# A new beginning for an attention and two-MLP kernel: other head pairs, loads on two queues, splits on three engines, the first group earlier

## The chip, the cores and the metric

The kernel runs on one core of one Trainium2 chip, as one program. The metric is the device time of that program in microseconds (us), the median of several runs. The engines are named as the profile names them: PE (TensorE), DVE (VectorE), ACT (ScalarE), POOL (GpSimd) and SP (SyncE, which here only issues DMAs).

## The reference

Attention with heads mixed before and after the softmax (batch 4, 12 heads, 448 positions, head size 64), then two MLPs (1792 tokens, 768 to 2048 to 768), all in float32:

```python
scores = scale * np.matmul(q, k.transpose(0, 1, 3, 2))
scores = np.einsum('bhij,hg->bgij', scores, w_pre)
scores = scores - np.max(scores, axis=-1, keepdims=True)
attn = np.exp(scores)
attn = attn / (np.sum(attn, axis=-1, keepdims=True) + 1e-09)
attn = np.einsum('bhij,hg->bgij', attn, w_post)
out = np.matmul(attn, v)
h = x @ w_in                       # first MLP, x is out with heads side by side
g = np.where(h > 0.0, h, np.exp(np.minimum(h, 0.0)) - 1.0)
h = (g @ w_out) @ w_in2            # second MLP
y = np.maximum(h, 0.0) ** 2 @ w_out2
```

## The kernel before

A float32 operand is split in two parts, a rounded one (hi, float32r) and the remainder (lo = x - hi), and a product is made of three matmuls on the parts (two where one side is stacked). So every operand costs a copy to float32r and a subtraction before PE can use it.

The queries of a batch are cut in four chunks of 12, 11, 11 and 11 groups; a group is ten query rows with all twelve heads, 120 partitions. Four batches make 16 chunks and 180 groups. For a chunk n, `first_scores` (batch 0, two heads at a time in the two halves of the PE rows) or `scores` (later batches) writes score rows to PSUM, and copies bring them to the tile `sc[n]`. For a group t these steps follow, each on the engine named:

- `gather(t)`: SP issues a DMA from `sc[n]` to `graw`, which puts the 120 rows of the group together. It needs all twelve heads of the chunk. `graw` has 5 buffers.
- `split(t)`: ACT casts to `gh`, POOL (DVE for the first two groups) subtracts to `gl`.
- `mix_pre(t)`: three matmuls mix the heads. `maxima(t)`: DVE takes the negative maximum, ACT the exponential with its sum into `tot`.
- `weigh(t)`: for two groups at once DVE adds 1e-9 to `tot`, takes the reciprocal and scales the mixing weights `wg`.
- `mix_post(t)`: four matmuls, and DVE copies the result to `at`. `values(n, i)` multiplies by `v` when all groups of a chunk are in `at`.

The order is written out by hand (`manual_schedule`); each engine takes its instructions in program order. In step t of the loop at the end of `attention` stand the gather of group t + 9, the copies of finished scores, the split of t + 6, the maxima of t + 3, `mix_pre` of t + 4, scores of a later chunk, `mix_post` of t, and other work put beside it by the table `extra` (loads of k, q and v, splits of k and q, values). Every DMA of the kernel is issued by SP, and it takes the lane of the eighth DMA before it, for whose end it waits.

Ahead of the loop stands the beginning, which the change rewrites: 16 matmuls on a zero tile `idle`; loads of the keys of batch 0 (`k_room`) and of the queries of chunks 0 and 1 (`q_room`); for the six head pairs of chunk 0 the splits of k and q on DVE, the scores, and two copies by ACT; nine gathers; the same for chunk 1; the mixing weights (`prepare_mixes`); then splits, `mix_pre` and `maxima` of the first groups. `load_odd` writes a 0/1 pattern to DRAM and reads it back across partitions; `split_k` uses it. After attention the MLPs run, PE alone nearly without a pause.

Of the kernel before, what the change touches and what calls it, by code (L numbers as in the profile page):

```python
# [7 lines left out]
F32 = mybir.dt.float32  # L8
# [42 lines left out]
def attention(tc, dram, psum, qr, kr, vr, w_pre, w_post, diagonal, xd, mlps):  # L51
    nc = tc.nc
    with ExitStack() as ctx:
# [21 lines left out]
        def load_odd():  # L75
            for a in range(2):
                nc.gpsimd.memset(turns[:, :, a : a + 1], float(a))
            nc.sync.dma_start(out=turns_d, in_=turns.rearrange("o d a -> o (d a)"))
            nc.sync.dma_start(out=odd, in_=turns_d.rearrange("o p -> p o"))
# [37 lines left out]
        k_room = work.tile([128, 3, 2, S], F32, name="k_room", tag="at", bufs=2)  # L117
        q_room = work.tile([128, 2, H // 2, CH], F32, name="q_room", tag="v", bufs=3)
# [14 lines left out]
        def split_first_k(p):  # L133
            j, a = divmod(p, 2)
            if a == 0:
                k0[j] = [key_tile() for _ in "hl"]
            raw, (hi, lo) = k_room[:, j, a, :], (x[:, a, :] for x in k0[j])
            nc.vector.tensor_copy(hi, raw)
            nc.vector.tensor_tensor(lo, raw, hi.bitcast(F32), ALU.subtract)

        def first_q(n, i, raw=None):
            raw = q_room[:, n, 3 * i : 3 * i + 3, :] if raw is None else raw
            at = (n * H + 6 * i) * CH
            src = qr[0, :, at : at + 6 * CH].rearrange("d (p a i) -> d a p i", p=3, a=2)
            for a in range(2):
                nc.sync.dma_start(out=raw[64 * a : 64 * a + 64], in_=src[:, a])
# [8 lines left out]
        def split_first_q(n, i, engine=nc.gpsimd):  # L155
# [35 lines left out]
        def load_v(b, i):  # L191

            vt[b, i] = work.tile([NJ, JC, DM // 2], F32, name="v", bufs=3)
            src = vr[b].rearrange("j (c d) -> j c d", c=JC)
            nc.sync.dma_start(out=vt[b, i], in_=src[:, :, i * DM // 2 : (i + 1) * DM // 2])
# [583 lines left out]
```

## Time and profile before

| | us |
|---|---|
| median of 3 runs | 1390.31 (1389.82 to 1390.93) |
| the profiled execution | 1388.04 |
| its span | 1386.0 |

| engine | busy us | share of the span | instructions |
|---|---|---|---|
| PE | 1366.1 | 99% | 8764 |
| DVE | 865.1 | 62% | 1812 |
| ACT | 703.8 | 51% | 1578 |
| POOL | 304.1 | 22% | 285 |

Busy shares are means over the whole span. PE is the engine that is nearly always busy; an engine with a smaller share can still be the one waited for in some stretch, and that is read from the rows of that stretch. All times in rows count from the start of the span.

### The profile page before, as it was taken

Reading aid. Unit: us, or ns where it says so; the run is one execution under the profiler, and the core shown is the slowest. Engines: PE = TensorE matmul, PEld = TensorE weight load, DVE = VectorE, ACT = ScalarE, POOL = GpSimd, SP = SyncE. Lnnn points to the kernel's source line nnn. Section 1 sums busy time; section 2 is a strip of 40 time slices with the busy share of each in tenths; the row PEclk is TensorE's granted clock in tenths of the full one; section 3 lists DMA queues with packets and bytes.
Section 4 is the critical chain, followed back from the end, with each engine's and each line's share of the span. In section 5 each row is a group of like instructions: output and inputs, shape, how many; then the busy total and the mean of one; then the engine's idle time right before and its main releaser. Section 6 shows DMA issues by size and latency. Waiting matters only on the chain.

```text
span 1386.0 us, 23859 instructions
## 1 busy us (share of the span) xinstructions
PE 1366.1 (99%) x8764; PEld 1270.2 (92%) x8764; DVE 865.1 (62%) x1812; ACT 703.8 (51%) x1578; POOL 304.1 (22%) x285
## 2 busy tenths in 40 slices
PE   7999999999999999999999999999999999999998
PEld 4789999999987999999999999999999999999998
DVE  5777778878788799866599997634441223443121
ACT  5777877878766577532255553225551113443111
POOL 2776876777657000000000000000000000000000
PEclk8999999999999999999999999999999999999999
DMA  4744744753735455544355576532112111112131
GB/s 130 212 142 145 214 159 140 211 177 129 202 123 163 153 171 163 193 173 161 131 170 163 164 236 210 176 120 58 54 65 61 61 42 51 52 53 62 41 108 41
DMA packets 116217, 182.92 MB, mean 132 GB/s; under 512 B 26660, under 2 KB 94597, under 8 KB 116101
## 3 DMA queue, kind: packets, MB, share of 16 engines
q1 hardware_dynamic: 116101, 181.41, 41.3%
q8 instruction: 69, 1.13, 0.3%
q14 instruction: 47, 0.39, 0.1%
HBM read 106.48 MB, written 36.18 MB: 103 GB/s over the span
## 4 chain that ended last, share of the span: by engine, by line
PE 93%; DVE 2%; DMA 2%; ACT 1%; SPq 1%; POOL 1%; issue 1%; POOLq 0%; DVEq 0%; ACTq 0%
PE ps_post L288 9%; PE ps_mix L644 8%; PE ps_mix L646 8%; PE ps_mix L645 8%; PE ps_qk L646 6%; PE ps_post L646 6%; PE ps_post L644 6%; PE ps_qk L644 6%; PE ps_qk L645 6%; PE ps_post L645 6%; PE ps_pv L314 5%; PE ps_pv L646 3%; PE ps_pv L645 3%; PE ps_pv L644 3%; PE ps_mix L252 3%; PE ps_mix L254 2%
## 5 line engine op out<-in xcount | busy, mean ns | idle before, releaser
L525 ACT CAST wh<-wf 128x384 fp32r<-128x384 f32 (+1 forms) x240 | 126.8, 533 | 272.4 <-DVE wf L508 113.5
L532 DVE TENSOR_TENSOR wl<-wf,wh 128x384 fp32r<-128x384 f32 (+1 forms) x240 | 138.7, 581 | 157.2 <-ACT wh L525 153.3
L246 POOL TENSOR_TENSOR gl<-graw,gh 120x448 fp32r<-120x448 f32 x178 | 203.0, 1145 | 130.1 <-ACT gh L245 125.7
L288 PEld LDWEIGHTS ps_post<-wg,ex 120*112 120x112 f32 x1440 | 173.5, 178 | 18.2 <-issue 4.7
L288 PE MATMUL ps_post<-wg,ex 120*112 120x120 f32 x1440 | 180.4, 268 | 3.3 <-DVE wg L277 1.6
L264 ACT ACTIVATE ex<-ps_mix,nmax 120x448 f32<-120x448 f32 x180 | 117.6, 653 | 42.0 <-DVE nmax L260 41.9
L294 DVE COPY at<-ps_post 112x480 f32<-112x480 f32 x160 | 104.4, 653 | 35.6 <-PE ps_post L288 34.8
L245 ACT CAST gh<-graw 120x448 fp32r<-120x448 f32 x180 | 105.7, 590 | 27.7 <-POOL gl L246 9.3
L260 DVE TENSOR_REDUCE nmax<-ps_mix 120x1 f32<-120x448 f32 x180 | 111.0, 617 | 8.5 <-PE ps_mix L254 8.5
L644 PE MATMUL ps_mix<-xh,wh 128*128 128x448 f32 x288 | 104.5, 363 | 0.0
L645 PE MATMUL ps_mix<-xl,wh 128*128 128x448 f32 x288 | 104.4, 362 | 0.0
L646 PE MATMUL ps_mix<-xh,wl 128*128 128x448 f32 x288 | 104.4, 362 | 0.0
L302 ACT COPY sc<-ps_qk 120x448 f32<-120x448 f32 x168 | 86.3, 545 | 27.9 <-PE ps_qk L229 24.5
L252 PE MATMUL ps_mix<-gh,pre_l 120*120 120x448 f32 x180 | 81.5, 453 | 4.6 <-ACT gh L245 3.8
L666 DVE TENSOR_TENSOR tmp<-tmp 128x448 f32<-128x448 f32 x64 | 39.9, 624 | 69.8 <-ACT tmp L665 69.8
L314 PE MATMUL ps_pv<-at,v 112*64 112x110 f32 (+2 forms) x1488 | 78.2, 262 | 0.6 <-DVE at L296 0.6
L484 ACT ACTIVATE wf<-wd 128x384 f32<-128x384 f32 (+1 forms) x120 | 69.3, 578 | 15.2 <-DMA wd<-w1i 8.6
L314 PEld LDWEIGHTS ps_pv<-at,v 112*64 112x64 f32 x1488 | 71.6, 137 | 4.4 <-DVE at L296 0.8
L670 DVE TENSOR_TENSOR hl<-tmp,hh 128x448 fp32r<-128x448 f32 x128 | 74.1, 619 | 0.4
L508 DVE SCALAR_TENSOR_TENSOR wf<-wd,wf 128x384 int32<-128x384 int32 (+1 forms) x120 | 70.9, 591 | 4.1
L506 DVE SCALAR_TENSOR_TENSOR wf<-wd,wf 128x384 int32<-128x384 int32 (+1 forms) x120 | 70.3, 586 | 4.1
L644 PE MATMUL ps_post<-xh,wh 128*128 128x448 f32 x192 | 69.6, 362 | 0.0
(161 smaller groups left out, 3404.3 us busy)
## 6 DMA issues: line engine op xcount, KB each, us to landing
graw<-sc SPq DMA_DIRECT2D x180, 210.0 KB
wd<-w1i SPq DMA_DIRECT2D x32, 384.0 KB
wd<-w1o SPq DMA_DIRECT2D x24, 512.0 KB
wd<-w2i SPq DMA_DIRECT2D x32, 384.0 KB
wd<-w2o SPq DMA_DIRECT2D x32, 384.0 KB
qraw<-qr SPq DMA_DIRECT2D x48, 180.0 KB
kraw<-kr SPq DMA_DIRECT2D x36, 224.0 KB
w1if<-wf SPq DMA_DIRECT2D x32, 192.0 KB
```

Of the source, the lines that this page charges most:

```text
L245: nc.scalar.copy(hi, x)
L246: engine.tensor_tensor(lo, x, hi.bitcast(F32), ALU.subtract)
L252: nc.tensor.matmul(p, pre_l, hi, start=True, stop=False)
L260: nc.vector.tensor_reduce(nmax, p, AX.X, ALU.max, negate=True)
L264: nc.scalar.activation(e, p, AF.Exp, bias=nmax, scale=1.0, accum_out=tot[t // 2][:, t % 2 : t % 2 + 1])
L288: nc.tensor.matmul(p[:, c, :], e[:, c * NJ : (c + 1) * NJ], w, start=True, stop=True)
L314: nc.tensor.matmul(pv[n][o : o + 64, i % 3, :w], vt[b, i // 3][:, jc, g % 6 * D : (g % 6 + 1) * D], at[n][:, jc, g, :w], start=(jc == 0), ...
L525: nc.scalar.copy(hi, f)
L532: self.nc.vector.tensor_tensor(lo, self.single.pop(i), hi.bitcast(F32), ALU.subtract)
L644: mm(p, wh, xh, start=first, stop=False)
L645: mm(p, wh, xl, start=False, stop=False)
L646: mm(p, wl, xh, start=False, stop=last)
```

## The change

- Chunk 0 to 3 of batch 0: the two heads computed together are p and p + 6, where they were 2p and 2p + 1. So each half of a load is one contiguous piece of the source, and several pairs go in one DMA.
- The first four pairs of loads are issued half by SP and half by ACT. The queries of chunk 1 are loaded ahead of the mixing matrices, and the read-back of `odd` moves behind the first nine gathers.
- The splits of the beginning go to three engines: ACT casts the queries of chunk 0, POOL subtracts for them, for one key pair and for half of chunk 1's queries; DVE does the rest.
- Matmuls on `idle` stand ahead of head pairs 1 to 5 of chunk 0 (two each) and ahead of `mix_pre` 0 to 3 (5, 2, 2, 2): 21 in all. `idle` takes a buffer of `ex` and no longer one of `graw`.
- Of chunk 1, four head pairs come ahead of the first group; pairs 4 and 5 stand between the first groups' steps. `mix_post(0)` is ahead of the loop.
- `weigh` adds 1e-9 to each sum by an instruction of its own (one column); the weights of groups 0 and 1 are made one by one.
- `v` of a batch is loaded in 8 DMAs of a quarter each in 8 steps, where there were 2 whole ones in two steps.

```diff
-        def first_k(j, pairs):
-            src = kr[0, :, 4 * j * S : (4 * j + 4) * S].rearrange("d (p a j) -> d a p j", p=2, a=2)
-            for x, y in pairs:
-                for a in range(2):
-                    nc.sync.dma_start(out=k_room[64 * a : 64 * a + 64, j, x:y], in_=src[:, a, x:y])
+        def first_k(x, y, queues=(nc.sync, nc.sync)):
+            for a in range(2):
+                src = kr[0, :, (6 * a + x) * S : (6 * a + y) * S].rearrange("d (p j) -> d p j", j=S)
+                queues[a].dma_start(out=k_room[64 * a : 64 * a + 64, x:y, :], in_=src)
...
-            (nc.vector.tensor_copy if n < 2 else nc.scalar.copy)(hi, raw)
+            copy(hi, raw)
...
-        def load_v(b, i):
+        def load_v(b, i, c):
...
-            nc.sync.dma_start(out=vt[b, i], in_=src[:, :, i * DM // 2 : (i + 1) * DM // 2])
+            at = c * DM + i * DM // 2
+            nc.sync.dma_start(out=vt[b, i][:, c, :], in_=vr[b][:, at : at + DM // 2])
...
+            for _ in range(warm):
+                nc.tensor.matmul(banks[0], idle[:64, :128], idle[:64], start=True, stop=True)
...
-            nc.vector.tensor_scalar_add(both, both, 1e-9)
+            for i in range(n):
+                nc.vector.tensor_scalar_add(sums[:, i : i + 1], sums[:, i : i + 1], 1e-9)
...
-                put(first[n] + 3, load_v, b, 0)
-                put(first[n] + 4, load_v, b, 1)
+                for j in range(JC):
+                    put(first[n] + 2 * j + (1 if b == 0 else -4), load_v, b, 0, j)
+                    put(first[n] + 2 * j + (2 if b == 0 else 4), load_v, b, 1, j)
...
-        first_k(0, ((0, 1),))
-        first_q(0, 0)
-        first_k(0, ((1, 2),))
-        first_k(1, ((0, 2),))
+        two = nc.sync, nc.scalar
+        first_k(0, 1, two)
+        first_q(0, 0, queues=two)
+        first_k(1, 2, two)
+        first_k(2, 4, two)
         first_q(0, 1)
-        first_k(2, ((0, 2),))
+        first_k(4, 6)
+        for i in range(2):
+            first_q(1, i)
         load_mixes()
-        load_odd()
-        first_q(1, 0)
-        first_q(1, 1)
+        spread_turns()
+        split_first_q(0, 0)
         for p in range(6):
-            split_first_k(p)
-            if p % 3 == 0:
-                split_first_q(0, p // 3, nc.vector)
-            first_scores(0, p, tags[p % 4], (act, act), True)
+            split_first_k(p, nc.gpsimd if p == 4 else nc.vector)
+            if p == 1:
+                split_first_q(0, 1)
+            if p == 5:
+                split_first_q(1, 0, nc.vector, dve)
+                split_first_q(1, 1, nc.gpsimd, dve)
+            first_scores(0, p, tags[p % 4], (act, act), True, 2 if p else 0)
         for t in range(AHEAD):
             gather(t)
-        split_first_q(1, 0, nc.vector)
-        split_first_q(1, 1, nc.vector)
-        for p in range(6):
-            first_scores(1, p, tags[(p + 2) % 4], (act, act if p % 2 else dve), True)
+        load_odd()
         prepare_mixes()
-        for t in range(2):
-            split(t, nc.vector)
-        for t in range(MIX):
-            mix_pre(t)
-            if t < MAX:
-                maxima(t)
-            split(t + 2)
-        weigh(0)
+        for p in range(4):
+            first_scores(1, p, (("mix", "mix"), ("mix", "post"), ("post", "pv"), ("qk", "qk"))[p], (act, dve), True)
+        split(0, nc.vector)
+        split(1, nc.vector)
+        mix_pre(0, 5)
+        split(2)
+        split(3)
+        maxima(0)
+        mix_pre(1, 2)
+        maxima(1)
+        weigh_first(0)
+        first_scores(1, 4, ("post", "pv"))
+        mix_pre(2, 2)
+        split(4, nc.vector)
+        weigh_first(1)
+        mix_post(0)
+        keep_scores()
+        maxima(2)
+        first_scores(1, 5)
+        mix_pre(3, 2)
+        split(5)
```

ACT at the very start, before: it loads its table and then only copies scores (`sc_143` is chunk 0, L216 the copies).

```order
L216 ACT_TABLE_LOAD
L216 COPY sc_143<-ps_qk_144 120x448
L216 COPY sc_143<-ps_qk_145 120x448
L216 COPY sc_143<-ps_mix_156 120x448
L216 COPY sc_143<-ps_mix_157 120x448
```

The same place now (`sc_142` is chunk 0, L159 the cast of queries).

```order
L132 DMA k_room_91<-kr 64x448
L147 DMA q_room_92<-qr 64x360
L132 DMA k_room_91<-kr 64x896
L159 ACT_TABLE_LOAD
L159 CAST qp_134<-q_room_92 128x360
L221 COPY sc_142<-ps_qk_143 120x448
L221 COPY sc_142<-ps_qk_144 120x448
L159 CAST qp_155<-q_room_92 128x360
L221 COPY sc_142<-ps_mix_159 120x448
```

Four DMA issues (one of `k_room` 64x448 is left out as a repetition) and a cast stand ahead of the first copy, and a second cast behind the second copy.

ACT between the last copies of chunk 0 and the first exponential, before (`sc_248` is chunk 1, `graw_222` the first group, L245 the casts of groups).

```order
L216 COPY sc_143<-ps_mix_213 120x448
L216 COPY sc_248<-ps_post_249 120x448
L216 COPY sc_248<-ps_mix_259 120x448
L216 COPY sc_248<-ps_pv_260 120x448
L216 COPY sc_248<-ps_qk_269 120x448
L216 COPY sc_248<-ps_mix_279 120x448
L216 COPY sc_248<-ps_mix_280 120x448
L216 COPY sc_248<-ps_post_289 120x448
L216 COPY sc_248<-ps_mix_299 120x448
L216 COPY sc_248<-ps_pv_300 120x448
L245 CAST gh_316<-graw_222 120x448
L245 CAST gh_320<-graw_224 120x448
```

The same place now (`sc_265` is chunk 1, `graw_239` the first group, L250 the casts, L272 the exponentials).

```order
L221 COPY sc_142<-ps_mix_228 120x448
L221 COPY sc_265<-ps_mix_266 120x448
L221 COPY sc_265<-ps_mix_276 120x448
L221 COPY sc_265<-ps_post_286 120x448
L221 COPY sc_265<-ps_qk_296 120x448
L250 CAST gh_306<-graw_239 120x448
L250 CAST gh_310<-graw_241 120x448
L250 CAST gh_323<-graw_243 120x448
L250 CAST gh_327<-graw_245 120x448
L272 ACTIVATE ex_333,tot_334<-ps_mix_314,nmax_331 120x448
L272 ACTIVATE ex_344,tot_334<-ps_mix_336,nmax_342 120x448
L250 CAST gh_365<-graw_247 120x448
```

Nine copies of chunk 1 stood between the last copy of chunk 0 and the first group's cast; now there are four, and four casts stand ahead of the first exponential where there were two.

SP in steps 1 to 6 of the loop, before (`graw` is a gather, `kraw`, `qraw` and `v` are loads).

```order
L238 DMA graw_402<-sc_143 120x1x448
L162 DMA kraw_434<-kr 128x1x448
L238 DMA graw_436<-sc_143 120x1x448
L146 DMA qraw_456<-qr 64x3x120 x2
L238 DMA graw_459<-sc_248 120x1x448
L195 DMA v_491<-vr 112x4x384
L238 DMA graw_493<-sc_248 120x1x448
L162 DMA kraw_522<-kr 128x1x448
L195 DMA v_524<-vr 112x4x384
L238 DMA graw_526<-sc_248 120x1x448
```

The same place now.

```order
L243 DMA graw_427<-sc_142 120x1x448
L163 DMA kraw_459<-kr 128x1x448
L197 DMA v_461<-vr 112x384
L243 DMA graw_463<-sc_142 120x1x448
L147 DMA qraw_483<-qr 64x360 x2
L197 DMA v_486<-vr 112x384
L243 DMA graw_488<-sc_265 120x1x448
L197 DMA v_461<-vr 112x384
L243 DMA graw_522<-sc_265 120x1x448
L163 DMA kraw_551<-kr 128x1x448
L197 DMA v_486<-vr 112x384
L243 DMA graw_554<-sc_265 120x1x448
```

Between two gathers stands at most a quarter of a `v` tile, where a whole one stood twice; there are more issues in all.

## Rows read from the trace of the kernel before

**Rows 1.** Windows: start:end, length, busy of five engines, PE clock, DMA share, GB/s

```profile
0.00:60.00 60.00, 49.51 (x272) 33.48 (x273) 37.48 (x88) 38.31 (x90) 25.17 (x29) 0.89 0.61 170
60.00:1386.00 1326.00, 1316.62 (x8494) 1236.70 (x8492) 827.59 (x1725) 665.48 (x1489) 278.94 (x256) 1.00 0.41 130
```

**Rows 2.** Timeline of PE: start, length, what, idle before and its releaser

```profile
1.32 5.44 PE L376 MATMUL ps_pv<-idle 128*128 128x512 bf16 x16 [1.32 <-POOL idle L373]
...
6.70 0.88 PE L212 MATMUL ps_qk<-kp,qp 64*120 64x448 f32 x6
...
22.79 0.46 PE L252 MATMUL ps_mix<-gh,pre_l 120*120 120x448 f32 x1 [1.69 <-ACT gh L245]
...
29.71 0.73 PE L252 MATMUL ps_mix<-gh,pre_l 120*120 120x448 f32 x1 [0.81 <-ACT gh L245]
...
35.65 0.49 PE L252 MATMUL ps_mix<-gh,pre_l 120*120 120x448 f32 x1
...
36.38 0.98 PE L288 MATMUL ps_post<-wg,ex 120*112 120x120 f32 x8
...
37.82 0.98 PE L288 MATMUL ps_post<-wg,ex 120*112 120x120 f32 x8
...
39.34 0.87 PE L212 MATMUL ps_qk<-kp,qp 64*120 64x448 f32 x6
40.14 1.07 PE L288 MATMUL ps_post<-wg,ex 120*112 120x120 f32 x8
...
62.27 2.68 PE L314 MATMUL ps_pv<-at,v 112*64 112x120 f32 x48
```

**Rows 3.** Windows of one microsecond: length, busy PE, its clock, DMA share, GB/s

```profile
3.00:4.00 1.00, 1.00 (x4) 1.00 0.66 174
9.00:10.00 1.00, 0.24 (x2) 1.00 1.00 217
26.00:27.00 1.00, 0.94 (x2) 0.50 0.38 136
36.00:37.00 1.00, 1.00 (x10) 1.00 0.93 210
```

**Rows 4.** Timeline of SP's queue: issues of DMAs

```profile
0.75 1.25 SPq L131 DMA_DIRECT2D k_room<-kr  x2
...
16.54 12.36 SPq L238 DMA_DIRECT2D graw<-sc  x9
...
38.43 0.63 SPq L195 DMA_DIRECT2D v<-vr  x1
```

**Rows 5.** Timeline of DVE

```profile
4.13 0.39 DVE L138 CAST kp<-k_room 128x448 fp32r<-128x448 f32 x1 [4.13 <-DMA k_room<-kr]
...
28.36 0.16 DVE L272 TENSOR_SCALAR tot<-tot 120x2 f32<-120x2 f32 x1
...
28.76 0.58 DVE L277 TENSOR_SCALAR wg<-post,rec 120x120 f32<-120x120 f32 x2
```

**Rows 6.** Timeline of ACT

```profile
0.74 1.28 ACT L216 ACT_TABLE_LOAD   x1 [0.74 <-PEq L770]
...
15.54 0.97 ACT L216 COPY sc<-ps_mix 120x448 f32<-120x448 f32 x2
...
22.09 1.10 ACT L245 CAST gh<-graw 120x448 fp32r<-120x448 f32 x2
...
24.61 0.63 ACT L264 ACTIVATE ex<-ps_mix,nmax 120x448 f32<-120x448 f32 x1 [1.42 <-DVE nmax L260]
```

**Rows 7.** Timeline of POOL

```profile
25.86 2.23 POOL L246 TENSOR_TENSOR gl<-graw,gh 120x448 fp32r<-120x448 f32 x2 [24.43 <-ACT gh L245]
...
35.50 0.96 POOL L159 TENSOR_TENSOR qp<-qraw,qp 128x360 fp32r<-128x360 f32 x1 [1.33 <-ACT qp L158]
```

**Rows 8.** DMA rate in 40 slices of 15 to 20 us

```profile
GB/s 238 215 92 15 81 142 254 211 39 50 100 161 219 169 96 69 161 211 185 54 0 0 0 0 215 229 229 287 244 244 229 258 272 244 229 287 244 229 244 272
```

**Rows 9.** Chain of waits, 36 to 50 us

```profile
39.16 7.18 DMA graw<-sc
```

More of the change, by code (lines that the diff above doesn't have):

```diff
@@ L136, in split_first_k, with first_q @@
                 k0[j] = [key_tile() for _ in "hl"]
-            raw, (hi, lo) = k_room[:, j, a, :], (x[:, a, :] for x in k0[j])
+            raw, (hi, lo) = k_room[:, p, :], (x[:, a, :] for x in k0[j])
             nc.vector.tensor_copy(hi, raw)
[L139 to L144, printed above, removed]
+            engine.tensor_tensor(lo, raw, hi.bitcast(F32), ALU.subtract)
+        def first_q(n, i, raw=None, queues=(nc.sync, nc.sync)):
+            raw = q_room[:, n, i, :, :] if raw is None else raw
             for a in range(2):
-                nc.sync.dma_start(out=raw[64 * a : 64 * a + 64], in_=src[:, a])
+                at = (n * H + 6 * a + 3 * i) * CH
+                src = qr[0, :, at : at + 3 * CH].rearrange("d (p i) -> d p i", p=3)
+                queues[a].dma_start(out=raw[64 * a : 64 * a + 64], in_=src)
             qraw[n, i] = raw
@@ L201, in score_tile, with first_scores @@
             sc[n] = score[(n + 1) % 2].tile([CH, H, S], F32, name="sc", bufs=1)
-        def first_scores(n, p, tags=("qk", "qk"), copies=(nc.scalar.copy, nc.scalar.copy), now=False):
+        def first_scores(n, p, tags=("qk", "qk"), copies=(nc.scalar.copy, nc.scalar.copy), now=False, warm=0):
             if p == 0:
                 score_tile(n)
-            out = [bank(psum, tag)[:CH, :S] for tag in tags]
+            banks = [bank(psum, tag) for tag in tags]
+            out = [x[:CH, :S] for x in banks]
+            for _ in range(warm):
+                nc.tensor.matmul(banks[0], idle[:64, :128], idle[:64], start=True, stop=True)
             h, l = 0, 1
@@ L215, in first_scores @@
                 for a in range(2):
-                    copies[a](sc[n][:, 2 * p + a, :], out[a])
+                    copies[a](sc[n][:, 6 * a + p, :], out[a])
             else:
-                taken.extend((sc[n][:, 2 * p + a, :], out[a]) for a in range(2))
+                taken.extend((sc[n][:, 6 * a + p, :], out[a]) for a in range(2))
         def scores(n, h):
@@ L247, in split, with mix_pre @@
             parts[t] = hi, lo
-        def mix_pre(t):
-            p = bank(psum, "mix")[:120, :S]
+        def mix_pre(t, warm=0):
+            p = bank(psum, "mix")
+            for _ in range(warm):
+                nc.tensor.matmul(p, idle[:, :128], idle, start=True, stop=True)
+            p = p[:120, :S]
             hi, lo = parts.pop(t)
@@ L267, in weigh, with weigh_first, weigh_some @@
         def weigh(t):
-            if t % 2 or t >= T:
-                return
-            both = tot.pop(t // 2)
-            nc.vector.tensor_scalar_add(both, both, 1e-9)
+            if t % 2 == 0 and t < T:
+                weigh_some(t, tot.pop(t // 2))
+        def weigh_first(t):
+            weigh_some(t, tot[0][:, t : t + 1])
+        def weigh_some(t, sums):
+            n = sums.shape[1]
+            for i in range(n):
+                nc.vector.tensor_scalar_add(sums[:, i : i + 1], sums[:, i : i + 1], 1e-9)
             rec = work.tile([120, 2], F32, name="rec", bufs=2)
-            nc.vector.reciprocal(rec, both)
-            for i in range(2):
+            nc.vector.reciprocal(rec[:, :n], sums)
+            for i in range(n):
                 w = work.tile([120, 120], F32, name="wg", bufs=4)
```

19 lines of the change are left out of this document (10 added, 9 removed).

## The prediction

> **What bounds the kernel now.** I read four things in turn. First the windows: from 60 us to the end PE is busy 1316.6 of 1326.0 us at a granted clock of 1.00, in the first 60 us only 49.5 and at 0.89 [rows 1]. So the change can win only in the first 60 us, and what it wins there comes off the end whole, as long as PE finds its work ready afterwards; 9.4 us of idling is all that is left behind 60 us. Second, PE's timeline of the beginning, for stations that both kernels pass: 16 idle matmuls to 6.76, the first scores at 6.70, the first `mix_pre` at 22.79 behind a wait for ACT's cast, `mix_pre(4)` at 29.71, `mix_pre(6)` at 35.65, and `values` of chunk 0 at 62.27 [rows 2]. Third, the other engines at those stations, to see what they wait for. Fourth, the windows of single microseconds: PE is granted 0.50 (1.2 of 2.4 GHz) at 26 us, 3 us behind the wait of 1.69 that ended at 22.79, and has 1.00 again at 36 us [rows 2, 3]. `mix_pre(4)` to `mix_pre(6)` is the PE work of two groups; it took 5.94 us, where a group at full clock takes 37.82 - 36.38 = 1.44 us [rows 2]. So the low clock costs 5.94 - 2.88 = 3.1 us there.
>
> I add up four stretches, each from one station to the next, on the profiled execution's clock.
>
> **Stretch 1, to the end of chunk 0's copies.** Before: ACT's last two copies start at 15.54 and take 0.97, end 16.51 [rows 6]. Now ACT first issues four loads. An issue by SP took 0.62 (two in 1.25) and the pair landed at 4.13, 2.13 after the second issue's end [rows 4, 5]; ACT's own issues are not in the trace, and I take the same 0.62. The first queries are then issued by 2.0 on both queues and land at about 4.1. The table load waits for them, 1.28, to 5.4; the cast takes at most 0.55 (two of 448 columns took 1.10), to 5.95 [rows 6]; POOL's subtraction 0.96, to 6.9 [rows 7]. PE is busy with idle matmuls to 6.76 anyway, and the first pair takes 0.88 [rows 2]: its end stays near 7.6. From there ACT makes six pairs of copies of 0.97 and one more cast, 6.4 us, and with 0.05 allowed between instructions it ends at 14.3. PE keeps that pace: two idle matmuls and a pair. An idle matmul took 0.34 on average [rows 2], mostly at low clock; at full clock I estimate 0.21, and 0.43 + 0.60 stays near 0.97. The loads keep it too, just: DMA moved 174 GB/s at a share of 0.66 at 3 us, where one queue issued, and 217 at 1.00 at 9 us [rows 3]; the second queue fills the first stretch and no more, so the last keys come about 1 us earlier than before. Gain 16.5 - 14.3 = 2.2. Bounds: nothing, if loads or ACT's issues are slower than SP's, and 2.2.
>
> The Trainium skill ("ScalarE: Activation LUTs", What ACT_TABLE_LOAD costs) counts 1.28 us for the load and 1.38 more for a drain, 2.66. The row shows 1.28, as the page has it; ACT then waited, so a drain could hide behind it. With the drain the first pair would come 1.2 us later and the gain be 1.0.
>
> **Stretch 2, to the cast of group 0.** Before: 16.51 to 22.09, 5.6 us, because ACT had its nine copies of chunk 1 ahead of the cast [rows 6]. The data were there long before: the gather was issued at 16.54 [rows 4], its bytes began to move at 18.0 and five gathers moved at about 250 GB/s [rows 8], so 0.86 us each, and the first was complete by 18.9; with 0.2 for its signal that is 2.5 us after the issue. Now ACT has four copies ahead, 2.1 us, which fit beneath those 2.5. DVE's four lie beside them. Gain 3.1; the cast starts at 16.8. Bounds: 2.0 if the landing takes a microsecond more, 3.4.
>
> **Stretch 3, to `mix_pre(6)`.** Before 13.6 us (22.09 to 35.65). Now four casts stand ahead of the first exponential, and the fourth group lands 3 x 0.86 later, at 19.4: cast to 20.0, exponential 0.63 [rows 6] to 20.6, add, reciprocal and first weights 0.7 (28.36 to 29.05 [rows 5]) to 21.3. PE does `mix_post(0)` (0.82 of the 1.44) to 22.1, pair 5 of chunk 1 (0.80, 39.34 to 40.14 [rows 2]), idle matmuls and two `mix_pre` by 24.6. The longer branch runs over ACT: DVE's second weights and maximum 2 to 23.5, exponential 24.1, cast 5 24.7, POOL 1.12 [rows 7] to 25.9, and over two copies and cast 6 at 26.2 POOL again to 27.3. So `mix_pre(6)` lies at 27.1 rather than 35.65, 10.3 us behind the cast. Gain 3.3, which is nearly the 3.1 of the low clock: with 11 idle matmuls PE has no pause above 1 us in my chain. Bounds: 0, if the clock falls as before, and 4.
>
> **Stretch 4, to `values` of chunk 0.** Before 62.27 - 35.65 = 26.6. The PE work in it is 12 groups of 1.44 and six pairs of 0.80, 22.1, so 4.5 were lost. The chain names the loss: a gather of 39.16 took 7.18 us to land [rows 9], with a whole `v` tile issued just ahead of it at 38.43 [rows 4] and DMA at a share of 0.93 at 36 us [rows 3]. Quarters of `v` let the gathers pass: in my count the gather of group 14 has 0.7 MB less ahead of it, near 3 us at 250 GB/s. POOL, with 1.12 a group and 0.96 or 1.12 for each part of k and q, is late by some 0.8 in all, and I leave 1.2 for pairs whose halves wait for a copy. Gain 2.5. Bounds: 0 and 4.5; the six extra SP issues of a batch, 3.7 us, have no wait ahead of them to fill and must fit between gathers.
>
> **Behind it.** 24 more `v` issues, 89 more adds. An add took 0.16 [rows 5], 14 us of DVE in all, which is 62% busy; PE found two groups back to back at 36.38 and 37.82 without a wait, so I count nothing. Were DVE on the path of each pair of groups it would be those 14 us; less than nothing is excluded, since nothing is taken away. The cover is the three groups by which the maxima run ahead.
>
> **Sum.** 2.2 + 3.1 + 3.3 + 2.5 = 11.1. I take 1.1 off for the beginning, half of stretch 1, since three of its prices (ACT's issues, POOL's first work, DVE and POOL side by side) stand in no row: 10.0. The profiled execution took 1388.04, 2.04 above its span; the median lies 2.27 above that. 1390.3 - 10.0 = 1380.3.
>
> **Rivals.**
> - *The low clock comes back.* If group 0 lands a microsecond or two later, PE has idle matmuls for 1 us and then nothing, as at 22 us before [rows 2]. Then stretch 3 loses the 3.1 again: 1383.4. For it: the loads and POOL's prices are guessed. Against it: 21 idle matmuls where before there were none.
> - *SP or DMA decides in stretch 4.* Steps 0 to 8 of the loop now hold 25 issues (9 gathers, 8 of k and q, 8 of `v`), 15.5 us at 0.62, in steps whose PE work is 9 x 1.44 + 4 x 0.80 = 16.2. If the extra issues of 3.7 us push the gathers back, 3.7 of the gain goes: 1384.0. Against it: SP begins 8 us earlier too, and in my count gathers are there two to three microseconds ahead of their casts.
> - *POOL is not ready.* Its first subtraction ran at 25.86, 24.43 us behind its last memset [rows 7]; the order has an ISA row, which loads a library, between the two. No row says when that was over. Now POOL is wanted at 5.95, and PE's first pair, ACT's copies and all else wait for it, microsecond for microsecond. Ready at 16 us the whole gain is gone, from 19 us on the kernel is slower by over 0.2%, and at 25.86 it would be 1400. The Trainium skill ("GPSIMD Engine Reference", 2.1 Instruction dispatch) names about 6 us for such a load, without a visible instruction: from 1.43 that is 7.4, 1.5 us late, 1381.8. The trace neither agrees nor disagrees.
> - *The second queue gives nothing*, loads as late as before: 2.2 less at most, 1381.4 after what I took off already.
>
> **How the numbers follow.** The forecast 0.62, with its own 1377.5 to 1382.5; the low clock 0.13; SP or DMA 0.16; POOL 0.09, of it 0.04 later than 16 us. Below 1377.5 lie cases with all gains at their upper bounds (2.2 + 3.4 + 4 + 4.5 = 14.1, 1376.2), to which I give 0.07. I end the range at 1385.5, above the two middle rivals. 0.2% is 2.8 us, about what a measurement of this kernel can tell from no change. Faster by more: 0.91. Within: 0.05, two rivals together or POOL ready near 16 us. Slower: 0.04, POOL alone.
>
> **What would show it.** In the new profile: chunk 0's last copy ends near 14.3; ACT casts group 0 near 16.8; `mix_pre(6)` stands near 27 and PE is granted 1.00 from 6 us on; `values` of chunk 0 starts near 51; behind it PE's idle time is again near 9 us. Stretch 1 is wrong if POOL's first subtraction starts much behind 6; stretch 3 if a window near 20 to 27 us shows 0.50; stretch 4 if ACT's casts again wait for gathers by more than 1 us. The whole is wrong if PE idles more behind 60 us by what it saved ahead of it.

## The result, and the profile after

| | before, us | after, us |
|---|---|---|
| median | 1390.32 (1389.82 to 1390.93, 4 runs) | 1372.8 (1371.55 to 1373.94, 4 runs) |
| the profiled execution | 1388.04 | 1373.31 |
| its span | 1386.0 | 1371.5 |

The ratio is 0.9874 (95% interval 0.9857 to 0.9891). I had forecast 1380.3, in a range of 1377.5 to 1385.5: the sign was right, and the gain of 17.5 us is 7.5 more than I had counted. In some executions of several kernels, before among them, the MLPs took about 11 us longer (944 to 945 us in four of the profiles below, 932.6 to 933.5 in all others), and as such runs weigh on medians and on ratios alike, the runs without them are named where they decide.

The windows of after, beside [rows 1] (start:end, length, busy of five engines, PE clock, DMA share, GB/s; the third row is the microsecond that had the low clock in [rows 3]):

```profile
0.00:60.00 60.00, 54.86 (x393) 39.34 (x396) 41.56 (x104) 44.51 (x104) 34.88 (x38) 1.00 0.63 192
60.00:1371.50 1311.50, 1305.03 (x8397) 1230.64 (x8393) 796.40 (x1795) 661.37 (x1476) 273.87 (x250) 1.00 0.41 131
...
26.00:27.00 1.00, 1.00 (x9) 0.57 (x8) 0.93 (x5) 0.28 (x1) 0.00 (x0) 1.00 0.48 185
```

The first 60 us are at a clock of 1.00 (0.89 before), and 26 to 27 us has 1.00 where it had 0.50. Behind 60 us PE idles 6.5 us in place of 9.4.

PE's timeline of after, at the stations of [rows 2] (start, length, what, idle before and its releaser):

```profile
1.32 4.95 PE L391 MATMUL ps_pv<-idle 128*128 128x512 bf16 x16 [1.32 <-POOL idle L388]
6.84 0.67 PE L217 MATMUL ps_qk<-kp,qp 64*120 64x448 f32 x4 [0.56 <-ACT qp L159]
...
19.67 0.47 PE L260 MATMUL ps_mix<-gh,pre_l 120*120 120x448 f32 x1 [0.53 <-ACT gh L250]
...
30.79 0.44 PE L260 MATMUL ps_mix<-gh,pre_l 120*120 120x448 f32 x1
...
54.57 0.63 PE L328 MATMUL ps_pv<-at,v 112*64 112x120 f32 x8
```

ACT, SP and POOL of after at the stations of [rows 6], [rows 4] and [rows 7]:

```profile
5.00 1.28 ACT L159 ACT_TABLE_LOAD   x1 [5.00 <-DMA q_room<-qr]
6.29 0.49 ACT L159 CAST qp<-q_room 128x360 fp32r<-128x360 f32 x1
...
14.67 0.97 ACT L221 COPY sc<-ps_mix 120x448 f32<-120x448 f32 x2
...
19.05 0.56 ACT L250 CAST gh<-graw 120x448 fp32r<-120x448 f32 x1 [0.69 <-DMA graw<-sc]
21.53 0.56 ACT L250 CAST gh<-graw 120x448 fp32r<-120x448 f32 x1 [1.91 <-DMA graw<-sc]
...
15.66 2.50 SPq L243 DMA_DIRECT2D graw<-sc  x3
...
6.86 0.95 POOL L160 TENSOR_TENSOR qp<-q_room,qp 128x360 fp32r<-128x360 f32 x1 [5.42 <-ACT qp L159]
```

So the four stretches gave 0.87 (chunk 0's copies end at 15.64), 2.17 (group 0's cast is at 19.05 in place of 22.09), 1.82 (`mix_pre(6)` is at 30.79 in place of 35.65) and 2.84 (`values` of chunk 0 is at 54.57 in place of 62.27). That is 7.7 us where the sum had 11.1, and 10.0 after the deduction.

The other half comes later, between chunk 0 and chunk 15. Here is `values` of chunk 15, the last of the attention, first before and then after:

```profile
453.44 2.44 PE L314 MATMUL ps_pv<-at,v 112*64 112x108 f32 x48 [0.63 <-DVE at L296]
```

```profile
438.06 2.44 PE L328 MATMUL ps_pv<-at,v 112*64 112x108 f32 x48 [0.63 <-DVE at L310]
```

From chunk 0 to chunk 15 it took 391.17 us before and 383.49 after: 7.7 us less, 2.8 of them by chunk 12 and 4.9 in the last three. The rest of the span, nearly all MLPs, is 0.9 longer (933.4 against 932.6). 7.7 + 7.7 - 0.9 = 14.5, the difference of the spans. The remaining 3 us of the 17.5 lie between profiled executions and medians: before's profile was 2.3 below its median, after's 0.5 above.

What changed there is seen in the groups of DVE, before and after (line, engine, operation, tiles, shapes, count, busy us and mean ns of one, idle before):

```profile
L272 DVE TENSOR_SCALAR tot<-tot 120x2 f32<-120x2 f32 x90 | 47.2, 525 | 1.5 <-ACT ex L264 1.5
```

```profile
L286 DVE TENSOR_SCALAR tot<-tot 120x1 f32<-120x1 f32 x180 | 18.6, 144 | 0.8 <-ACT ex L272 0.8
```

Twice as many adds took 28.6 us less. My price of 0.16 was one row of [rows 5], at 28.36, and just there POOL did nothing: its pair from 25.86 on was over at 28.09 [rows 7]. Where POOL works, the two-column add is held. In before, 58 of the 90 adds took more than 0.2 us, and each of the 58 ended 0.02 to 0.03 us behind the end of one of POOL's subtractions; the 19 beside which POOL did nothing took at most 0.17. The dearest case of before, DVE, then POOL, then PE:

```profile
441.60 2.24 DVE L272 TENSOR_SCALAR tot<-tot 120x2 f32<-120x2 f32 x1
443.88 0.17 DVE L274 RECIPROCAL rec<-tot 120x2 f32<-120x2 f32 x1
...
441.57 1.15 POOL L246 TENSOR_TENSOR gl<-graw,gh 120x448 fp32r<-120x448 f32 x1
442.67 1.15 POOL L639 TENSOR_TENSOR xl<-tmp,xh 128x448 fp32r<-128x448 f32 x1
...
444.56 1.04 PE L288 MATMUL ps_post<-wg,ex 120*112 120x120 f32 x8 [1.40 <-DVE wg L277]
```

The add ends at 443.84, when POOL's second subtraction ends (443.82); reciprocal and weights follow, and PE waited 1.40 for them. It is the only add of before that was held over two subtractions: the other 57 ended with the one that was running, in 34 cases with POOL's next already begun. After, beside a pair of POOL's, two adds of one column take 0.20 together (DVE, then POOL):

```profile
408.01 0.20 DVE L286 TENSOR_SCALAR tot<-tot 120x1 f32<-120x1 f32 x2
408.25 0.17 DVE L288 RECIPROCAL rec<-tot 120x2 f32<-120x2 f32 x1
...
407.94 2.38 POOL L251 TENSOR_TENSOR gl<-graw,gh 120x448 fp32r<-120x448 f32 x2 [1.01 <-PE ps_mix L261]
```

Late weights are not the only way by which the held adds reach PE. PE's waits from 60 to 560 us, before and then after (total us, times, longest):

```profile
PE ps_qk L228 <- ACT sc L302: 1.9, 2, 1.4
PE ps_post L288 <- DVE wg L277: 1.6, 2, 1.4
PE ps_post L288 <- ACT at L297: 1.4, 2, 0.9
PE ps_pv L314 <- DVE at L296: 0.6, 1, 0.6
```

```profile
PE ps_post L302 <- ACT at L311: 1.2, 2, 0.9
PE ps_pv L328 <- DVE at L310: 0.6, 1, 0.6
```

The largest item of before stands ahead of score matmuls (`ps_qk`). Its longest wait, 1.36, came through ACT, whose exponential had waited for DVE's maximum (ACT, then PE):

```profile
404.62 0.63 ACT L264 ACTIVATE ex<-ps_mix,nmax 120x448 f32<-120x448 f32 x1 [2.19 <-DVE nmax L260]
...
405.82 0.47 PE L228 MATMUL ps_qk<-kp,qp 128*120 128x448 f32 x1 [1.36 <-ACT sc L302]
```

### The profile page after: what moved, and what is told of

Read it like the earlier page. It is cut to its first block, busy times and chain, and to the rows that moved or that the text cites. A ratio compares the mean times of both kernels' runs of the same rounds, so it can differ in the third digit from the quotient of the medians.

```text
span 1371.5 us, 24022 instructions
## 1 busy us (share of the span) xinstructions
PE 1359.9 (99%) x8784; PEld 1270.0 (93%) x8785; DVE 838.0 (61%) x1899; ACT 705.9 (51%) x1579; POOL 308.8 (23%) x288
## 4 chain that ended last, share of the span: by engine, by line
PE 97%; DMA 1%; DVE 0%; POOL 0%; issue 0%; ACT 0%; ACTq 0%; SPq 0%; POOLq 0%; DVEq 0%
PE ps_post L302 10%; PE ps_mix L674 8%; PE ps_mix L676 8%; PE ps_mix L675 8%; PE ps_post L676 6%; PE ps_post L675 6%; PE ps_post L674 6%; PE ps_qk L675 6%; PE ps_qk L676 6%; PE ps_qk L674 6%; PE ps_pv L328 6%; PE ps_mix L260 3%; PE ps_pv L675 3%; PE ps_pv L676 3%; PE ps_pv L674 3%; PE ps_mix L262 3%
## 5 line engine op out<-in xcount | busy, mean ns | idle before, releaser
L272 ACT ACTIVATE ex<-ps_mix,nmax 120x448 f32<-120x448 f32 x180 | 118.4, 658 | 21.7 <-DVE nmax L268 19.6
L250 ACT CAST gh<-graw 120x448 fp32r<-120x448 f32 x180 | 106.6, 592 | 32.2 <-POOL qp L188 11.6
L675 PE MATMUL ps_post<-xl,wh 128*128 128x448 f32 x192 | 69.6, 362 | 0.0
```

The lines of the kernel that those rows point to most:

```text
L250: nc.scalar.copy(hi, x)
L272: nc.scalar.activation(e, p, AF.Exp, bias=nmax, scale=1.0, accum_out=tot[t // 2][:, t % 2 : t % 2 + 1])
L675: mm(p, wh, xl, start=False, stop=False)
```

## The experiments

Each kernel's three stations come from its trace: the first cast of a group (ACT), the start of `values` of chunk 0, and the time from there to `values` of chunk 15 (PE). The range behind a median is that of its runs. A ratio is to runs of before that were taken with them on the same chip. The rows come from several chips, between which before itself moved by up to 2 us, so medians from different chips that lie within 2 us are not told apart.

| kernel | first cast | chunk 0 | chunk 0 to 15 | median, us |
|---|---|---|---|---|
| before | 22.09 | 62.27 | 391.17 | 1390.32 |
| after | 19.05 | 54.57 | 383.49 | 1372.8 |
| x1_before_one_add | 21.70 | 61.41 | 383.44 | 1381.12 (1379.30 to 1383.46) |
| x5_before_reversed | 23.08 | 63.04 | 383.48 | 1380.72 (1378.89 to 1392.23) |
| x4_before_three_columns | 23.03 | 64.16 | 390.95 | 1388.5 (1386.66 to 1401.04) |
| x2_after_joint_add | 18.49 | 52.42 | 392.16 | 1382.44 (1379.79 to 1393.20) |
| z3_after_no_adds | 19.00 | 55.13 | 382.81 | 1371.4 (1370.73 to 1373.10) |
| x3_after_whole_v | 19.26 | 58.25 | 383.48 | 1374.81 (1372.88 to 1376.93) |
| y1_after_no_pool | 19.55 | 55.02 | 383.59 | 1373.11 (1371.11 to 1374.71) |
| y2_after_sp_loads | 19.36 | 53.12 | 383.53 | 1372.11 (1371.46 to 1382.46) |
| y3_after_no_idle | 18.43 | 53.88 | 383.56 | 1372.39 (1371.82 to 1374.85) |
| z2_after_three_undone | 19.45 | 55.38 | 383.46 | 1372.37 (1371.52 to 1373.93) |
| z1_after_six_pairs | 19.37 | 53.29 | 383.48 | 1373.85 (1372.11 to 1383.47) |
| w1_after_late_queries | 20.20 | 54.33 | 383.64 | 1373.37 (1372.38 to 1376.11) |
| w2_before_early_queries | 20.12 | 59.26 | 383.40 | 1379.22 (1377.04 to 1391.43) |
| w3_before_queries_v | 20.41 | 57.98 | 383.47 | 1382.09 (1375.63 to 1387.57) |
| w4_order_and_v | 22.04 | 56.91 | 383.57 | 1374.98 (1372.81 to 1375.15) |
| w5_old_group_order | 19.83 | 57.72 | 383.47 | 1375.94 (1374.81 to 1388.87) |

The fourth column has two levels, 391 to 392 with the joint add and 383.5 without, whatever the beginning. The third shows how far one profile can be trusted: 61.4 to 64.2 for before's beginning, 52.4 to 55.4 for the changed one (after, x2, y1 to y3, z1 to z3 and w1; some of these undo a part of it).

### The add

**x1_before_one_add**

```diff
-            nc.vector.tensor_scalar_add(both, both, 1e-9)
+            for i in range(2):
+                nc.vector.tensor_scalar_add(both[:, i : i + 1], both[:, i : i + 1], 1e-9)
```

> The kernel before with one change alone: 1e-9 is added to each sum by its own instruction of one column. Theory (lock): an add over two columns that DVE starts while POOL subtracts is held until POOL ends (0.70 us against 0.16), one column is not; it explains what was won behind chunk 0's values, so about 1390.3 - 7 = 1383 (1381 to 1386), adds at 0.14 us each, values of chunk 0 still near 62. Rival (beginning): all of the gain comes from the earlier start, and its growth afterwards is another alignment of the engines: 1390 to 1391.

The ratio to before is 0.9923 (0.9894 to 0.9952). Against the 21 of the 24 runs of before beside it that lie below 1393 (median 1388.77) it is 7.65 faster. Chunk 0 to 15 fell from 391.17 to 383.44, the amount that after gained. The low clock of the beginning stayed. PE between these stations, in two windows each (to about chunk 12, then to chunk 15), before and then x1 (start:end, length, busy PE, its clock, DMA share, GB/s):

```profile
62.27:382.00 319.73, 319.23 (x2940) 1.00 0.55 169
382.00:453.44 71.44, 66.07 (x642) 1.00 0.43 137
```

```profile
61.41:378.00 316.59, 316.59 (x2937) 1.00 0.55 171
378.00:444.85 66.85, 64.78 (x645) 1.00 0.47 147
```

PE's idle time fell by 3.8 us only, from 5.87 to 2.07. The other 3.9 were hidden in rows that count as busy. By the starts of PE's rows, all that was lost up to chunk 12 lay at the score matmuls (61.5 us in before, 58.7 in x1, for 300 of them), while `mix_post` took the same 125.4 in both; in the last three chunks 3.1 lay at `mix_post` and 1.7 at the scores. Of these losses only the two waits of 1.4, at 405.82 and at 444.56, are followed back to DVE here.

**x2_after_joint_add**

```diff
-            for i in range(n):
-                nc.vector.tensor_scalar_add(sums[:, i : i + 1], sums[:, i : i + 1], 1e-9)
+            nc.vector.tensor_scalar_add(sums, sums, 1e-9)
```

> The changed kernel with the two sums of a pair added to by one instruction again. Theory (lock): about 1372.8 + 7 = 1380 (1377 to 1382), near the forecast of the beginning alone, adds at some 0.5 us in the mean. Rival (beginning): 1372 to 1374.

The ratio is 0.9953 (0.9924 to 0.9982). Eight of its twelve runs lie at 1379.79 to 1383.81 (median 1381.5), 8.7 above after. Its group of adds, and its dearest add beside POOL (DVE):

```profile
L285 DVE TENSOR_SCALAR tot<-tot 120x2 f32<-120x2 f32 (+1 forms) x91 | 51.1, 562 | 0.9 <-ACT ex L272 0.9
...
426.40 4.61 DVE L285 TENSOR_SCALAR tot<-tot 120x2 f32<-120x2 f32 x1
```

One add of two columns took 4.61 us, over four of POOL's subtractions that stand without a gap, and the weights then came late by 0.96. It is again the only one that was held over more than one. Of the adds held, 36 ended with a subtraction although POOL had already begun the next.

**x5_before_reversed** (x1 with the later sum first)

```diff
-            for i in range(2):
+            for i in (1, 0):
```

> The kernel before with one add a sum, the later group's sum first: DVE must wait for both exponentials ahead of either add, as the joint add does. Theory (lock): only the number of columns counts, so 1381 (1379 to 1384), as with the earlier sum first, and adds of 0.14 us. Rival (the wait for the second sum is what one add a sum takes away): 1387 to 1391.

The ratio is 0.9928 (0.9896 to 0.9960), as x1's: the gain isn't the earlier start on the first sum.

**x4_before_three_columns** (the joint add over a third column that holds a constant)

```diff
+        sums3 = [work.tile([120, 3], F32, name=f"sums{i}") for i in range(3)]
...
-                tot[t // 2] = work.tile([120, 2], F32, name="tot", bufs=3)
+                tot[t // 2] = sums3[t // 2 % 3]
```

> The kernel before with the joint add kept, but over three columns (the third is a constant that nothing reads). Theory (lock, and that an odd count of columns does not take the mode that needs POOL's port): adds at 0.16 us and the time of the kernel with one add a sum. Rival (it is the wait for the second sum that costs, since a joint add can't begin before both exponentials): adds and time as before, 1390 to 1391.

The ratio is 1.0004 (0.9976 to 1.0033): nothing was gained. DVE's group shows why:

```profile
L275 DVE TENSOR_SCALAR sums<-sums 120x3 f32<-120x3 f32 x90 | 48.8, 543 | 0.0
```

Three columns are held like two, so an odd count is no way out.

**z3_after_no_adds**

```diff
-            for i in range(n):
-                nc.vector.tensor_scalar_add(sums[:, i : i + 1], sums[:, i : i + 1], 1e-9)
```

> The changed kernel without the adds of 1e-9 to the sums of the softmax (a part of the computation as written; each sum holds the exponential of a maximum and is so at least 1). Theory (the one-column adds of 0.144 us are off the path by now, and VectorE only loses 18.6 us of busy time): 1371 to 1373 us, no change. Rival (even the short adds stand between the sum and the weights on the path): under 1371 us, by up to 0.16 us for each of the 90 groups.

The median is 1371.4, beside 1372.37 of z2 on the same chip, and the ranges overlap: the two are not told apart. Chunk 0 to 15 is 0.7 shorter. So of the 8.4 us that the joint adds cost in all (391.17 to 382.81), single columns had left 0.7.

### Parts of the beginning, undone one by one

**x3_after_whole_v**

```diff
-                for j in range(JC):
-                    put(first[n] + 2 * j + (1 if b == 0 else -4), load_v, b, 0, j)
-                    put(first[n] + 2 * j + (2 if b == 0 else 4), load_v, b, 1, j)
+                put(first[n] + 3, load_v, b, 0)
+                put(first[n] + 4, load_v, b, 1)
```

> The changed kernel with v loaded by two whole DMAs in steps 3 and 4 of a batch again. Theory (gathers stand behind v, stretch 4): ACT's casts wait for gathers again near 40 us, values of chunk 0 some 2 to 4 us later, 1375 to 1377. Rival (the earlier start alone lets the gathers run ahead far enough): 1372 to 1374.

The median is 1374.81, some 2 above after, with ranges that overlap, and the ratio is 0.9873 (0.9833 to 0.9913), as after's: the time alone shows no loss. The stations do. From `mix_pre(6)` to `values` of chunk 0 it took 27.1 us, where after needed 23.8 and before 26.6. ACT's waits for gathers from 20 to 100 us, x3 and then after (total us, times, longest):

```profile
ACT gh L249 <- DMA graw<-sc: 5.5, 4, 3.4
```

```profile
ACT gh L250 <- DMA graw<-sc: 2.4, 3, 1.9
```

The longest, 3.38 at 46.94, follows the whole `v` tiles that were issued at 34.40 and 36.68: the gathers come late behind them, as stretch 4 had it.

**y1_after_no_pool** (the beginning's subtractions on DVE)

```diff
-            split_first_k(p, nc.gpsimd if p == 4 else nc.vector)
+            split_first_k(p, nc.vector)
```

> The changed kernel with the subtractions of the beginning all on DVE (the four that POOL had). Theory (DVE's and POOL's subtractions hold each other up, 0.93 against 0.63 us): DVE's four more take 2.2 us and save 2.1 of holding, chunk 0's copies end within 0.7 of 15.64, time 1372 to 1374. Rival (three engines are worth what they seem): 1374 to 1376, copies end 1.5 to 2.5 later.

**y2_after_sp_loads**

```diff
-        two = nc.sync, nc.scalar
+        two = nc.sync, nc.sync
```

> The changed kernel with all loads issued by SP. Forecast of stretch 1: the second queue is worth about a microsecond of the last keys' landing: 1373.5 to 1375, chunk 0's copies end 0.5 to 1.5 later. Rival (loads are bound by the DMA engines anyway): 1372 to 1373.5.

**y3_after_no_idle** (no `warm` in pairs 1 to 5 of chunk 0 and in `mix_pre` 0 to 3)

```diff
-        mix_pre(0, 5)
+        mix_pre(0)
```

> The changed kernel without the 21 idle matmuls ahead of scores and mix_pre. Theory (they hold the clock): PE granted 0.50 somewhere between 10 and 35 us and 2 to 4 us more, 1375 to 1377. Rival (the shorter waits hold it): clock 1.00 and 1371 to 1373.

The three ratios are 0.9860 (0.9821 to 0.9900), 0.9868 (0.9823 to 0.9912) and 0.9859 (0.9816 to 0.9901): none of the three parts is worth anything that can be measured. Chunk 0's copies did end later without POOL (16.32) and without the second queue (16.49, where after has 15.64), but nothing of that is left in the time. Windows of y3 and of x1 at the place of the low clock:

```profile
25.00:30.00 5.00, 4.45 (x28) 3.47 (x27) 3.51 (x11) 4.72 (x13) 3.28 (x3) 1.00 0.52 165
```

```profile
25.00:30.00 5.00, 3.63 (x8) 2.01 (x8) 2.02 (x7) 3.39 (x9) 2.89 (x3) 0.53 0.39 146
```

Without the 21 idle matmuls y3 is granted 1.00 here, where x1, with before's beginning, has 0.53. Between the first scores and 30 us PE had four waits of 1.33 to 1.70 in x1, and in y3 a single one above a microsecond, 1.16, for the first cast. That the shorter waits kept the clock is only argued, as z2 shows next.

**z2_after_three_undone** (y1, y2 and y3 together)

> The changed kernel with three parts undone at once: all beginning loads through SP, the beginning's subtractions on VectorE alone, and no idle matmuls. Each of them alone was worth nothing. Theory (the order of the code, the pairs, the v quarters and the one add carry the whole gain): 1372 to 1374 us, granted clock 1.00 to 60 us. Rival (each part hid the loss of another, so that together they cost): 1375 us or more, with a lower clock before 40 us or group 0's cast after 21 us.

The median is 1372.37: in time they do not hide one another's loss either. But the theory also had the clock at 1.00 to 60 us, and with all three undone it fell again (z2; start:end, length, busy PE, its clock, DMA share, GB/s):

```profile
10.00:15.00 5.00, 3.83 (x20) 0.74 0.42 102
```

In z2 it stood at 0.50 from 13 to 15 us, behind a wait of 0.90 at 11.73 and none longer since the first scores. y1 and y2, which kept the idle matmuls, were at 1.00 there, and so was y3, which kept the other two parts. So the idle matmuls may have held the clock where the other parts were undone; but x3, which has them, was granted 0.76 from 20 to 25 us. What decides is open.

**z1_after_six_pairs**

```diff
-        for p in range(4):
-            first_scores(1, p, (("mix", "mix"), ("mix", "post"), ("post", "pv"), ("qk", "qk"))[p], (act, dve), True)
+        for p in range(6):
+            first_scores(1, p, tags[(p + 2) % 4], (act, act if p % 2 else dve), True)
```

> The changed kernel with chunk 1's pairs as before: all six pairs (five more than the four, with their copies, nine of them on ScalarE) stand ahead of the casts of the first groups, and none between groups. Theory (the copies ahead of the casts set when group 0's cast begins, as stretch 2 of the prediction said): the first cast moves from 19.05 to about 20.7 us, the values of chunk 0 from 54.57 to about 56, and the time is 1374.5 to 1376 us. Rival (the cast waits for its gather anyway, and only the later groups set the chain): 1372 to 1373.5 us.

The ratio is 0.9859 (0.9813 to 0.9905); four of its six runs lie at 1372.11 to 1374.66, as after. This refutes my cause for stretch 2. All nine copies are ahead of the cast again, and ACT reads (z1):

```profile
18.66 0.65 ACT L221 COPY sc<-ps_pv 120x448 f32<-120x448 f32 x1
19.37 0.56 ACT L250 CAST gh<-graw 120x448 fp32r<-120x448 f32 x1
```

They fit beneath the gather: the cast comes 0.3 behind after's. In before they did not, since they began late. DVE and PE of before:

```profile
16.62 0.35 DVE L158 CAST qp<-q_room 128x360 fp32r<-128x360 f32 x1 [2.35 <-DMA q_room<-qr]
...
17.11 0.94 PE L212 MATMUL ps_post<-kp,qp 64*120 64x448 f32 x6 [1.61 <-DVE qp L158]
```

The queries of chunk 1 stood on SP behind the mixing matrices and behind the write and read-back of `odd`, and were late by over 2 us.

### What carries the beginning

**w2_before_early_queries** (x1, and one more edit)

```diff
-        load_mixes()
-        load_odd()
         first_q(1, 0)
         first_q(1, 1)
+        load_mixes()
+        load_odd()
```

> The kernel before with one add per sum, and one part of the new beginning alone: the queries of chunk 1 are loaded ahead of the mixing matrices and odd. Theory: the wait of 2.0 to 2.4 us on VectorE for these queries goes, group 0's cast comes at about 20 us where it came at 21.70 with one add per sum, the values of chunk 0 near 59.5, and the time is 1378.5 to 1379.5 us, against 1381.1. Rival (the loads are not what holds chunk 1's pairs, or the low clock eats the gain): 1380.5 to 1382 us.

The ratio is 0.9943 (0.9920 to 0.9966). Nine of its twelve runs lie at 1377.04 to 1380.82, about 3 below x1 in the mean; x1 ran on another chip and the ranges overlap, so the size of this gain rests on the stations. The cast of the queries on DVE of w2, which stood at 16.62 in before:

```profile
14.07 0.34 DVE L158 CAST qp<-q_room 128x360 fp32r<-128x360 f32 x1
```

It no longer waits, and group 0's cast came at 20.12, 1.6 ahead of x1's.

**w3_before_queries_v** (w2 with `v` in quarters)

> The same with v in quarters, in the changed kernel's steps, as well. Theory (quarters are worth 2 us, the order of the first groups the rest): 1376.5 to 1378 us, values of chunk 0 near 57. Rival (these two parts carry all of the beginning's gain): 1372 to 1374.5 us.

The ratio is 0.9944 (0.9920 to 0.9968). Six of its twelve runs lie at 1375.63 to 1377.53, 1 to 2 below w2's nine, on the same chip. That is the theory's size, and `mix_pre(6)` to `values` of chunk 0 took 24.4 us against 26.2 in w2. About 3 are left to after.

**w1_after_late_queries** (z1 with the loads of chunk 1's queries moved back, and their splits on DVE behind the gathers)

```diff
-        for i in range(2):
-            first_q(1, i)
         load_mixes()
         spread_turns()
+        load_odd()
+        for i in range(2):
+            first_q(1, i)
```

> The changed kernel with all six pairs of chunk 1 ahead of the casts, and the queries of chunk 1 loaded behind the mixing matrices and behind the write and the read-back of odd, as before, their splits behind the gathers' place on VectorE. Theory (in the kernel before, chunk 1's pairs waited for these queries and pushed copies and casts back): PE waits over 1 us for the queries near 16 us again, group 0's cast moves to 21 to 22 us, and the time is 1375 to 1377 us. Rival (the order of loads is worth nothing, since the cast of group 0 waits for its gather to about 19 us and later groups catch up): 1372 to 1373.5 us.

The ratio is 0.9887 (0.9870 to 0.9903), the median 1373.37: the rival held. But it did not undo the whole lateness: DVE's cast of these queries waited 1.02 at 14.20, since four loads of the beginning go through ACT and SP reaches the queries sooner.

**w5_old_group_order** (z1 with before's order of the first four groups)

```diff
-        split(2)
-        split(3)
-        maxima(0)
...
+        for t in range(MIX):
+            mix_pre(t, (5, 2, 2, 2)[t])
+            if t < MAX:
+                maxima(t)
+            split(t + 2)
+        weigh(0)
```

> The changed kernel with all six pairs of chunk 1 ahead of the casts, and the order of the first four groups as before: two casts, an exponential, a cast, an exponential; the first two groups' weights made together, and mix_post(0) in the loop. Loads, engines, idle matmuls, v in quarters and one add a sum stay. Theory (the order is worth about 3 us): mix_pre(6) is 13 us or more behind the first cast, the values of chunk 0 near 56, and 1375 to 1377 us. Rival (the early loads and the clock kept by idle matmuls carry it): mix_pre(6) within 11.5 us of the cast and 1372 to 1374 us.

The ratio is 0.9922 (0.9895 to 0.9949), the median 1375.94, about 3 above after. The clock was 1.00 throughout the beginning, so it is not the clock. The time and chunk 0 (57.72) are the theory's, the station is the rival's: `mix_pre(6)` came 11.2 behind the cast. The loss is later, up to chunk 0's `values`, and through which wait I have not shown.

**w4_order_and_v** (late queries, SP's loads, DVE's subtractions, no idle matmuls, six pairs: all of it undone but the order, the quarters, one add a sum, the pairing and ACT's two casts of chunk 0's queries)

> The changed kernel with nearly all of the new beginning undone at once: queries of chunk 1 late, all loads through SP, subtractions of the beginning on VectorE, no idle matmuls ahead of pairs and mixes, all six pairs of chunk 1 ahead of the casts. Left are the new order of the first four groups, v in quarters, one add a sum, and heads 6 apart. Theory (the order of the first groups is enough by itself): mix_pre(6) within 11 us of the first cast and 1373 to 1375 us. Rival (the late queries now show, since nothing else is left to cover them): first cast after 21.5 us and 1375.5 to 1378 us.

The ratio is 0.9896 (0.9882 to 0.9910), the median 1374.98, 2 above after with ranges that overlap. The first cast came at 22.04, as in before, and yet `mix_pre(6)` 10.0 behind it, where before needed 13.6. PE was granted 0.60 from 12 to 20 us and 0.72 from 30 to 36, so a part of the 2 us can be the clock. The order of the first groups is most of what is left, and it covers late queries nearly whole.

## Why the prediction was wrong

**The step that failed** is *Behind it*: "An add took 0.16", "so I count nothing", and "less than nothing is excluded, since nothing is taken away". Something was taken away, the second column and with it the hold beside POOL. The adds, 180 in place of 90, gave back 7.7 us between chunk 0 and chunk 15 where the sum had nothing; x1 and x2 show it from both sides, x5 excludes the earlier first sum, x4 an odd count. The error was in reading one row of 0.16 as the price of 90; the group's mean in the same profile, 525 ns, says that most were not like it.

The first reading failed with it: "9.4 us of idling is all that is left behind 60 us", so that the change "can win only in the first 60 us". About half of the 7.7 was never idle time: it lay in rows of PE that count as busy, most of it at score matmuls (x1).

The cover that I named, maxima three groups ahead, did hold for the weights up to chunk 12, where `mix_post` lost nothing; the 2.8 us lost there came in by the scores, which the prediction did not look at. At the end of the attention, where POOL also subtracts for the MLPs, the weights were late too, by up to 1.40 behind the add of 2.24.

With 7.7 for that term my sum would have come out at 1372.6. That this is so near 1372.8 is partly luck: the beginning gave 2.3 less than forecast and the MLPs took 0.9 more, and the 3 us between profiles and medians made up for both. By the spans alone, 14.5 less, the median would be 1375.8, still below the range.

The Trainium skill has the rule, and I did not weigh it: "VectorE: DVE Perf Modes" (Mode 2×_2P) lets a `tensor_scalar` on SBUF use both of VectorE's port pairs when its outermost dimension longer than one is even, or equal in source and destination; "SBUF — State Buffer" (Who interferes with whom) makes the second pair an exclusive lock shared with GpSimd. The trace agrees for two columns (525 ns), three (543) and one (144). That one column has no such dimension to split is my reading of the rule. It does not fit every form: the weights' multiplication, a `tensor_scalar` on 3 x 40 elements in SBUF, is not held (333 ns in the mean beside POOL in before, 335 without).

**Stretch 1** gave 0.87, not 2.2. The queries landed at 5.00, not 4.1; the prediction's "mostly at low clock" for the idle matmuls is not what the rows say, which have 1.00 at 3 us [rows 3]; and DVE's subtractions are held beside POOL's (DVE, then POOL, of after):

```profile
9.91 1.33 DVE L140 TENSOR_TENSOR kp<-k_room,kp 128x448 fp32r<-128x448 f32 x1
...
11.88 1.45 DVE L140 TENSOR_TENSOR kp<-k_room,kp 128x448 fp32r<-128x448 f32 x1
...
9.80 0.96 POOL L160 TENSOR_TENSOR qp<-q_room,qp 128x360 fp32r<-128x360 f32 x1 [1.99 <-ACT qp L159]
11.62 1.23 POOL L140 TENSOR_TENSOR kp<-k_room,kp 128x448 fp32r<-128x448 f32 x1 [0.86 <-DVE kp L139]
```

They took 0.63 alone (4.18 and 6.04 of after). y1 shows that without POOL it is no better: DVE then has the work itself.

**Stretch 2** gave 2.17 of 3.1, by another cause (late queries, not nine copies), and the gather landed 3.4 behind its issue, not 2.5 (15.66 to the cast at 19.05, which waited for it); the 0.2 that the prediction gives to its signal stands in no row.

**Stretch 3** gave 1.82 of 3.3. Here the second gather came 1.91 late in after's profile; where it did not (x2, y3, z1), `mix_pre(6)` followed the first cast by 10.3 to 10.4, against 10.3 forecast. The low clock did go, and y3 shows that it does so without the idle matmuls ahead of pairs and mixes; z2 shows that this is not so in every setting.

**Stretch 4** gave 2.84, where 2.5 was forecast; the stations of x3, and of w3 beside w2, bear out the quarters of `v`.

So the beginning, 10.0 forecast, is 7.7 in after's profile and 6.9 to 9.9 over the nine profiles of the changed beginning that the table's third column puts together. Four profiles of before's beginning have 62.7 in the mean and these nine 54.1, which is 8.6. It was slightly oversized; the missing 7.7 were the adds.

**The rivals.** The low clock did not come back. SP's 24 further issues cost nothing visible. POOL was ready when wanted (its subtraction at 6.86 waited for ACT's cast, not for a library). The second queue indeed gave nothing in time (y2), but this rival's 1381.4 also counted nothing for the adds.

## What to carry to other kernels

Price an instruction that runs many times by its group's mean and by its slowest row, and ask what another engine did beside each; 525 ns in the group beside 160 ns in the row was the error of the failed term. A busy engine can still hide a wait: compare the time that the same rows take in two runs. A tiny `tensor_scalar` on VectorE that other work waits for is worth splitting into single columns when GpSimd works beside it. Undo parts singly and together: here the order of the first groups hides late loads (w1, w4), and only in before's order do early loads show (w2 beside x1).

## What the runs showed of the hardware

- The add over two columns is held until POOL's running subtraction ends: 58 of 90 in before took over 0.2 us and ended 0.02 to 0.03 behind such an end; over three columns 62 of 90 took over 0.2 (x4). One add in before and one in x2 were held over two subtractions (2.24) and over four (4.61); why these two is open. One column is free of it (0.13 to 0.15 in all 180 of after, 155 of them beside POOL); so is the reciprocal on the same two columns (166 ns mean in before, 166 in after).
- Gathers land unevenly. The second cast came 0.87 behind the first in x2, y2, y3 and z1, and about 2.5 in after, y1 and z3, with like loads ahead. The cause is open.
- PE held 1.00 through the beginning without the 21 idle matmuls in y3, but not in z2 (0.50 from 13 to 15 us); with them, early loads and the old order of groups it held 1.00 (w5), and with them, whole loads of `v` and the new order 0.76 from 20 to 25 us (x3). With the old order, late queries and no idle matmuls there, x1 had 0.53 from 25 to 30 us, nearly all at the lower level (1.2 of 2.4 GHz).
